# Attention from the 17th block on: one TensorE job per block for scores, query and probability transposes, and a PSUM bank that changes hands

## The chip, the core and the metric

The kernel runs on one core of one Trainium2 chip. The metric is the device time of one execution in microseconds (us); lower is better.

## What is computed

Three stages follow one another. The first is attention over `q`, `k`, `v` of shape (2, 8, 576, 64) that keeps only the 32 largest scores of each row:

```python
scores = scale * np.matmul(q, k.transpose(0, 1, 3, 2))
kth = np.partition(scores, -32, axis=-1)[..., -32:-31]
scores = np.where(scores >= kth, scores, -1e9)
attn = np.exp(scores - scores.max(-1, keepdims=True))
attn = attn / (attn.sum(-1, keepdims=True) + 1e-9)
x = np.matmul(attn, v)
```

The result is seen as 1152 tokens of width 512 (nine tiles of 128). The second stage is a mixture of 8 experts (512 to 1024, ReLU, back to 512), each token weighted by a matrix that eight row and column normalisations make of the gate logits. The third is a mixture of 8 experts in which each token goes to its best expert, with room for 288 tokens per expert. All numbers are float32.

## The kernel before

**A planner writes the order.** Each piece of work is a `Job` with an engine, a rank, a modelled cost, the jobs it depends on, and the buffers (`Box`es of a `Pool`) it takes and uses. `Order.run` (L147) plays the engines forward: it picks the job that can start first and, among those within 0.02 us, the one of lowest rank, and emits its instructions. Every engine then runs its instructions in that order on the chip. A job starts in the plan only when all the boxes in its `take` list are free at once.

**PSUM** has eight banks of 128x512 floats, in two pools (`places`, L297): `psa` for attention and all small work (its tiles are called `tp`), and `psm` for the experts' matmuls (`yp`; `psm` boxes are given out in the order in which they were made). They begin with four banks each. In `visits_first` (L998) one `psa` bank is handed to `psm` and never comes back, so from about 100 us on attention has three banks and the experts five; an expert matmul into that bank shows as `tp` in the profile.

**Attention** is cut into 72 blocks of 128 query rows against 576 keys, for one head (or 64 rows of two heads). Blocks 0 to 15 take another path; from block 16 (`ROWS`) a block n makes these jobs:

- TensorE transposes the query (`block`, one instruction by the helper `tr`, L257) into a bank of its own; ScalarE writes its high part (L598), VectorE the low part (L606). Before that the query is loaded by a DMA of the SP queue.
- Two TensorE jobs make the scores (L618), 288 columns each, each into its own bank; ScalarE copies each to `sc` (L623). Their rank is n-2.
- `search` (L709): VectorE finds the 32nd largest value by four MAX8 and three MATCH_REPLACE8 (L715, L719, L721). After the second round ScalarE writes the exponentials, in halves, into two PSUM banks (L728), and VectorE masks them into `e` (L730). ScalarE divides by the sum (L739).
- Two TensorE jobs transpose `e` (L257): four 128x128 pieces into one bank, the fifth piece into another, at rank n+1. ScalarE writes the high part (L769), VectorE (or GpSimd, for one block in six, later one in three, through a copy on ScalarE) the low part (L773, L777).

So a block has five TensorE jobs and takes seven banks in turn. After the last block of a pair of heads, `values` multiplies by `v` (L809), with one bank per head. `keys` takes two banks per pair.

**The first mixture** is cut into visits (expert, tiles t0 to t1), `visit` (L960). For each of eight slices f, layer 1 (L980) makes a hidden 128 x n tile in a `psm` bank; ScalarE and VectorE read it as two parts (L932, L934); layer 2 (L1090) accumulates into one `psm` bank per tile. The next slice's hidden bank is asked for ahead. The visits in `EARLY` need only tiles that attention has finished and are the work that TensorE does between attention jobs: first 256 columns (two tiles), then two visits of 384, one of 256, two of 512, one of 256. The visits in `LATE` wait for `gate`, which comes after the last block of attention and the gate's logits (L891 to L900); the normalisation (L1138 to L1162) follows.

Of the kernel before, what the change touches and what calls it, by code (L numbers as in the profile page):

```python
# [29 lines left out]
ROWS = 16  # L30
# [182 lines left out]
class Net:  # L213
# [10 lines left out]
    def __init__(self, ctx, tc, q, k, v, wg1, w11, w12, wg2, w21, w22, capacity, out):  # L224
        self.ctx, self.tc, self.nc = ctx, tc, tc.nc
        self.q, self.k, self.v, self.out = q, k, v, out
        self.wg1, self.w11, self.w12 = wg1, w11, w12
        self.wg2, self.w21, self.w22 = wg2, w21, w22
        self.cap = int(capacity)
        self.B, self.H, self.S, self.D = q.shape  # L230
        self.N = self.B * self.S
        self.NT = self.N // 128
        self.E = wg1.shape[1]
        self.F = w11.shape[2]
        self.DM = self.H * self.D
# [5 lines left out]
        self.ending = self.ended = self.fast = False  # L241
        Pool.all, Box.all = [], []


# [177 lines left out]
    def attention(self):  # L422
# [3 lines left out]
        self.khave, self.qhave = {}, {}  # L426
        n = 0
        self.attended = []
        for g, (b, tiles) in enumerate(GROUPS):
            made = []  # L430
            for pair in range(4):
# [12 lines left out]
                    self.block(x)  # L444
                    n += 1
                if n > ROWS:
                    made += self.values(b, pair, tiles, heads, n - 1)
# [4 lines left out]
            self.spans.append((c0, c1, made))  # L452
            for t in range(c0 // 128, -(-c1 // 128)):
                self.xdone.setdefault(t, []).extend(made)
        self.gate_logits()

    def keys(self, b, pair, n):

# [120 lines left out]
    def block(self, x):  # L579
        nc, b, t, pair, n = self.nc, x["b"], x["t"], x["pair"], x["n"]  # L580
        qg, jq = self.queries(b, t, pair, n)
        two = t == 4
        if n < 2:
            return self.block_full(x, qg, jq)
        qs = (self.qz if two else self.qs).box()
        p = self.psa.box()
        i = 0 if two else x["heads"][0]["i"]
        j = self.job("PE", n - 3.5, 0.13, lambda: self.tr(p.t[:, :128], qg.t[:, i].rearrange("p s d -> p (s d)")),
                     deps=[jq], take=[p, qs], use=[qg])

        def parts(s):
            if two:
                return qs.t[:, s].rearrange("p a (c d) -> p (a c) d", c=2)[:, ::3, :]
            return qs.t[:, s]

        def src():
            return p.t[:, :128].rearrange("p (a c) -> p a c", a=2) if two else p.t[:, :128]
        jh = self.job("ACT", n - 2.9, t_act(128), lambda: nc.scalar.activation(parts(0), src(), AF.Copy),  # L598
                      deps=[j], use=[p, qs])
        if 2 <= n < ALONE:  # L600
            jm = self.job("PE", n - 2.9, 0.12, lambda: nc.tensor.matmul(
                p.t[:, :128], self.minus, parts(0), start=False, stop=True, skip_group_check=True), deps=[jh], use=[p, qs])
            jl = self.job("ACT", n - 2.9, t_act(128), lambda: nc.scalar.activation(parts(1), p.t[:, :128], AF.Copy),
                          deps=[jm], use=[p, qs])
        else:
            jl = self.job("DVE", n - 2.4, t_dve(128), lambda: nc.vector.tensor_sub(  # L606
                parts(1), src(), parts(0).bitcast(F32)), deps=[jh], use=[p])
# [3 lines left out]
        got = []  # L611
        for half in range(2):
            ps = self.psa.box()

            def scores(half=half, ps=ps):
                for m, (s, k) in enumerate(terms):
                    w = qs.t[:, s, k, :] if two else qs.t[:, s]
                    nc.tensor.matmul(ps.t[:, :288], w, keys[k][0].t[:, half * 288:(half + 1) * 288],  # L618
                                     start=m == 0, stop=m == len(terms) - 1)
            j = self.job("PE", n - 2 + 0.1 * half, 0.14 * len(terms), scores,  # L620
                         deps=[jh, jl] + [d for _, dd in keys for d in dd], take=[ps] if half else [ps, sc],
                         use=[qs, sc] + [kb for kb, _ in keys])
            got.append(self.job("ACT", n - 1.9 + 0.1 * half, t_act(288), lambda half=half, ps=ps: nc.scalar.activation(  # L623
                sc.t[:, half], ps.t[:, :288], AF.Copy), deps=[j], use=[ps, sc]))
        (self.search_first if n < ROWS else self.search)(x, sc, got)

    def block_full(self, x, qg, jq):

# [80 lines left out]
    def search(self, x, sc, got):  # L709
# [33 lines left out]
        for t0, t1, rows in ((0, 4, 128), (4, 5, 64)):  # L743
            p, nt = self.psa.box(), t1 - t0

            def turn(p=p, t0=t0, t1=t1, rows=rows):
                for t in range(t0, t1):
                    self.tr(p.t[:rows, (t - t0) * 128:(t - t0 + 1) * 128], e.t[:, t * 128:t * 128 + rows])
            fresh = [hd["et"] for hd in heads if "et_done" not in hd]
            for hd in heads:  # L750
                hd.setdefault("et_done", [])
            j = self.job("PE", n + 1, 0.12 * nt, turn, deps=[jn], take=[p] + fresh, use=[e])

            def view(p=p, rows=rows, nt=nt):
                return p.t[:rows, :nt * 128].rearrange("p (t c) -> p t c", t=nt)
            dve = n >= ALONE and n % (EASY if n < 44 else 3)
            if not dve:
                er = self.er.box()

                def copied(er=er, rows=rows, nt=nt):  # L760
                    return er.t[:rows, :nt * 128].rearrange("p (t c) -> p t c", t=nt)
                jr = self.job("ACT", n + 0.6, t_act(128 * nt), lambda p=p, view=view, copied=copied:
                              nc.scalar.activation(copied(), view(), AF.Copy), deps=[j], take=[er], use=[p])
            for i, hd in enumerate(heads):
                def part(s, hd=hd, rows=rows, t0=t0, t1=t1):
                    if s and t0:
                        return hd["et"].t[0][64:, t0:t1, c0:c0 + w]
                    return hd["et"].t[s][:rows, t0:t1, c0:c0 + w]
                jh = self.job("ACT", n + 0.5, t_act(w * nt), lambda i=i, part=part, view=view: nc.scalar.activation(  # L769
                    part(0), view()[:, :, i * w:(i + 1) * w], AF.Copy), deps=[j], use=[p, hd["et"]])  # L770
                if dve:
                    jl = self.job("DVE", n + 0.5, t_dve(w * nt), lambda i=i, part=part, view=view:
                                  nc.vector.tensor_sub(part(1), view()[:, :, i * w:(i + 1) * w], part(0).bitcast(F32)),  # L773
                                  deps=[jh], use=[p])
                else:
                    jl = self.job("POOL", n, t_pool(w * nt), lambda i=i, part=part, copied=copied:
                                  nc.gpsimd.tensor_sub(part(1), copied()[:, :, i * w:(i + 1) * w],  # L777
                                                       part(0).bitcast(F32)), deps=[jh, jr], use=[er])
                hd["et_done"] += [jh, jl]

    def values(self, b, pair, tiles, heads, n):

# [215 lines left out]
    def visits_first(self, count):  # L998
# [26 lines left out]
        for e in range(count):  # L1025
# [741 lines left out]
```

## Time and profile before

| | us |
|---|---|
| median of 3 runs | 1178.45 (1178.33 to 1179.57) |
| the profiled execution's own time | 1180.55 |
| its span, first to last instruction | 1178.8 |
| TensorE busy in the span | 1157.3 (98%) |
| weight loads (PEld) busy | 1003.6 (85%) |
| VectorE busy | 912.8 (77%) |
| ScalarE busy | 734.2 (62%) |

Sums of time below are made against the profiled execution. PE is TensorE's matmuls, whose ends are modelled, so neighbours overlap in the profile and a wait shorter than an overlap does not show as idle; PEld is its weight loads, DVE VectorE, ACT ScalarE, POOL GpSimd, SP the engine whose queue issues most DMAs. PEclk is the granted TensorE clock, 1.00 being 2.4 GHz.

### The profile page before, as it was taken

The page shows a single profiled execution, that of the slowest core. Times are in us where ns is not written, and L with a number is a line of the kernel's source. Part 1 is how long each engine was busy: PE and PEld are TensorE (multiplying, and loading weights), DVE is VectorE, ACT ScalarE, POOL GpSimd, SP SyncE. Part 2 cuts the span into 40 slices and gives each one's busy share as a digit, 9 for nine tenths or more (in the row PEclk, how much of TensorE's full clock was granted, in tenths as well). Part 3 has the DMA queues.
Part 4 walks back from the last instruction along what each step waited for, and adds up shares of the span by engine and source line. Part 5 has one row for each costly group of instructions (what it writes and reads, how often), then busy time and mean ns, then how long its engine had stood idle before and what let it go on. Part 6 is the DMA issues. An engine that isn't in the chain of part 4 may idle for free.

```text
span 1178.8 us, 20927 instructions
## 1 busy us (share of the span) xinstructions
PE 1157.3 (98%) x6610; PEld 1003.6 (85%) x6610; DVE 912.8 (77%) x2194; ACT 734.2 (62%) x1729; POOL 421.2 (36%) x387
## 2 busy tenths in 40 slices
PE   8998999999999999999999999999999999999998
PEld 5876889888888888778888889989999999898886
DVE  7999999999999999995845668754455555568883
ACT  7656888989888978766443335543334444258882
POOL 5463788877556755445000001000000000016541
PEclk9999999999999999999999999999999999999999
DMA  5457765756444664434545555644444444279980
GB/s 142 113 152 196 203 192 174 200 168 165 142 128 113 188 193 131 152 113 147 170 153 180 160 156 185 195 138 122 129 125 143 143 134 135 72 232 359 352 265 23
DMA packets 243032, 194.04 MB, mean 165 GB/s; under 512 B 67487, under 2 KB 186271, under 8 KB 242912
## 3 DMA queue, kind: packets, MB, share of 16 engines
q1 hardware_dynamic: 240656, 187.74, 53.2%
q0 software_dynamic: 1648, 4.73, 1.0%
q8 instruction: 54, 0.88, 0.3%
q14 instruction: 66, 0.54, 0.1%
q10 hardware_dynamic: 608, 0.15, 0.1%
HBM read 172.34 MB, written 20.80 MB: 164 GB/s over the span
## 4 chain that ended last, share of the span: by engine, by line
PE 73%; DVE 15%; ACT 4%; issue 4%; DMA 2%; SPq 1%; POOL 1%; POOLq 0%; DVEq 0%; ACTq 0%
PE yp L980 24%; PE yp L1090 21%; PE tp L1090 6%; PE tp L980 4%; PE tp L257 3%; DVE wk L719 3%; DVE m L721 3%; PE yp L1309 2%; PE tp L618 2%; PE tp L809 2%; DVE wk L665 2%; PE yp L1325 2%; DVE e L730 1%; DVE m L667 1%; PE tp L1309 1%
## 5 line engine op out<-in xcount | busy, mean ns | idle before, releaser
L1718 POOL DMA_INDIRECT disp<-acc,idx x9 | 10.5, 1172 | 460.8 <-DVE run L1714 460.8
L924 POOL TENSOR_TENSOR w0l<-ra,w0h 128x512 fp32r<-128x512 f32 x96 | 124.3, 1295 | 70.8 <-ACT w0h L918 65.0
L924 POOL TENSOR_TENSOR w1l<-rb,w1h 128x512 fp32r<-128x512 f32 x96 | 124.1, 1293 | 61.8 <-ACT w1h L918 56.0
L980 PE MATMUL yp<-xl,w0h 128*128 128x256 f32 (+2 forms) x680 | 142.3, 331 | 0.0
L980 PE MATMUL yp<-xh,w0h 128*128 128x256 f32 (+2 forms) x680 | 141.7, 330 | 0.2 <-ACT w0h L918 0.2
L980 PE MATMUL yp<-xh,w0l 128*128 128x256 f32 (+2 forms) x680 | 141.6, 330 | 0.0
L918 ACT ACTIVATE w0h<-ra 128x512 fp32r<-128x512 f32 x211 | 131.8, 625 | 0.4 <-DMA ra<-in_moe_w_dram 0.3
L918 ACT ACTIVATE w1h<-rb 128x512 fp32r<-128x512 f32 x148 | 93.1, 629 | 55.4 <-PE yp L1090 47.6
L721 DVE MAX8 m<-wk 128x8 f32<-128x576 f32 x168 | 125.8, 756 | 1.0
L980 PEld LDWEIGHTS yp<-xh,w0h 128*128 128x128 f32 x680 | 113.9, 189 | 11.9 <-ACT w0h L918 0.5
L932 ACT ACTIVATE hh<-yp 128x256 fp32r<-128x256 f32 (+3 forms) x142 | 64.0, 450 | 94.8 <-PE yp L980 78.4
L980 PEld LDWEIGHTS yp<-xh,w0l 128*128 128x128 f32 x680 | 110.6, 189 | 6.5 <-POOL w0l L924 0.4
L980 PEld LDWEIGHTS yp<-xl,w0h 128*128 128x128 f32 x680 | 110.9, 190 | 6.0
L1090 PE MATMUL yp<-w1h,hh 128*128 128x512 f32 x280 | 114.3, 408 | 0.0
L934 DVE SCALAR_TENSOR_TENSOR hl<-yp,hh 128x256 fp32r<-128x256 f32 (+3 forms) x142 | 71.8, 506 | 53.5 <-ACT hh L932 52.7
L1090 PE MATMUL yp<-v,f 128*128 128x512 f32 x480 | 111.8, 391 | 0.0
L1090 PE MATMUL yp<-w1l,hh 128*128 128x512 f32 x280 | 110.1, 393 | 0.0
L1090 PE MATMUL yp<-w1h,hl 128*128 128x512 f32 x280 | 109.8, 392 | 0.0
L1090 PEld LDWEIGHTS yp<-v,f 128*128 128x128 f32 x480 | 89.6, 188 | 18.1
L918 ACT ACTIVATE v<-rb 128x512 fp32r<-128x512 f32 x65 | 40.6, 628 | 79.1 <-PE yp L1090 52.4
L719 DVE MATCH_REPLACE8 wk<-m,wk 128x576 f32<-128x576 f32 x112 | 83.7, 748 | 0.5
L921 DVE TENSOR_TENSOR w0l<-ra,w0h 128x512 fp32r<-128x512 f32 x115 | 79.1, 688 | 1.3 <-ACT w0h L918 0.3
(485 smaller groups left out, 2726.9 us busy)
## 6 DMA issues: line engine op xcount, KB each, us to landing
rb<-in_moe_w_dram SPq DMA_DIRECT2D x248, 256.0 KB
ra<-in_moe_w_dram SPq DMA_DIRECT2D x245, 256.0 KB
acc<-in_moe_w_dram SPq DMA_DIRECT2D x67, 256.0 KB
y<-ys SPq DMA_DIRECT2D x31, 256.0 KB
ys<-y SPq DMA_DIRECT2D x21, 256.0 KB
vr<-in_v_dram SPq DMA_DIRECT2D x40, 128.0 KB
disp<-z SPq DMA_DIRECT2D x6, 771.0 KB
qg<-in_q_dram SPq DMA_DIRECT2D x63, 64.0 KB
```

The lines of the kernel that those rows point to most:

```text
L257: self.nc.tensor.transpose(out, in_, self.ident[:p, :p])
L618: nc.tensor.matmul(ps.t[:, :288], w, keys[k][0].t[:, half * 288:(half + 1) * 288], start=m == 0, stop=m == len(terms) - 1)
L719: j = self.job("DVE", r, 0.73, lambda i=i: nc.vector.match_replace(wk.t, m.t[:, i], flat() if i == 0 else wk.t, LOW), deps=[j], take=[wk] ...
L721: j = self.job("DVE", r, 0.66, lambda i=i: nc.vector.max(m.t[:, i + 1], wk.t), deps=[j], use=[wk] if i == 2 else [])
L918: jh = self.job("ACT", -500 + rank, t_act(512, True), lambda r=r, w=w: nc.scalar.activation(w.t[0], r.t, AF.Copy), deps=[j], take=[w])
L921: jl = self.job("DVE", -100 + rank, t_dve(512, True), lambda r=r, w=w: nc.vector.tensor_sub(w.t[1], r.t, w.t[0].bitcast(F32)), deps=[jh], ...
L924: jl = self.job("POOL", -100 + rank if k > 8 * NATIVE + 4 else FIRST - 3, t_pool(512), lambda r=r, w=w: nc.gpsimd.tensor_sub(w.t[1], r.t, ...
L932: jh = self.job("ACT", -1000 + k * 0.001, t_act(b - a), lambda: nc.scalar.activation(h.t[0][:, a:b], p.t[:, :b - a], AF.Relu), deps=deps, ...
L934: jl = self.job("DVE", -1000 + k * 0.001, t_dve(b - a), lambda: nc.vector.scalar_tensor_tensor(h.t[1][:, a:b], p.t[:, :b - a], 0.0, h.t[0] ...
L980: nc.tensor.matmul(p.t[:, :b - a], w1[0].t[i][:, d, :], self.xt[s][:, d, c0 + a:c0 + b], start=m == 0 and d == 0, stop=m == 2 and d == 3)
L1090: nc.tensor.matmul(y[t].t, h.t[i][:, c:c + 128], w2[0].t[s], start=f == 0 and m == 0, stop=f == last and m == 2)
L1309: nc.tensor.matmul(p.t[:, :n], w1[0].t[i][:, d, :], hl.t[s][:, d, :n], start=m == 0 and d == 0, stop=m == 2 and d == 3)
```

## The change

From block 19 on, the TensorE work of a block is not five jobs but is collected into one job by a new method `together(m)`: the scores of block m+3 (both halves), the transpose of the query of block m+4, then the five transposes of `e` of block m. The job has all their dependencies and takes all their boxes at once. The query's transpose goes to columns 288 to 415 of the bank of the second half of the scores, the fifth transpose of `e` to the same columns of the bank of the first half. The job thus takes three banks, and a block five in all with the two of the exponentials, which stay in PSUM. The making of `values` is put off until the pair's last block has its job.

The bank that `psa` gives to `psm` in `visits_first` is given back at the end of `visits_first`; the first early visit of 512 columns takes it again. Between the two, attention has four banks and the experts four. The modelled cost of a transpose of `e` goes from 0.12 to 0.11 us. The instructions, their sizes and the DMAs stay the same.

```diff
+AHEAD = 3
+GROUPED = AHEAD + 1
...
+        for m in range(n - GROUPED, n):
+            self.together(m)
...
+    def together(self, m, query=None):
+        turn, rows = self.turns.get(m), self.rows_.pop(m + AHEAD, None)
+        if turn:
+            deps, take, use, cost, tail, _, jobs = turn
+            calls = []
+            tail.append(rows[2][0] if rows else self.psa.box())
+            take = take + ([] if rows else tail)
+            use = use + tail
+            if rows:
+                x, sc, ps, sdeps, stake, suse, scores, _ = rows
+                deps, take, use, cost = deps + sdeps, take + stake, use + suse, cost + 0.14 * 4 * len(x["heads"])
+                calls.append(scores)
+            go = jobs[0]
+            if query:
+                qdeps, qtake, quse, *_ = query
+                deps, take, use, cost = deps + qdeps, take + qtake, use + quse, cost + 0.13
+            def all_(calls=calls, go=go, query=query):
+                for f in calls:
+                    f()
+                if query:
+                    query[3]()
+                go()
+            j = self.job("PE", m, cost, all_, deps=deps, take=take, use=use)
...
@@ block
-        p = self.psa.box()
+        mine = n >= ROWS + GROUPED
+        p, at = (None, 288) if mine else (self.psa.box(), 0)
...
+        if n < ROWS + AHEAD:
...
+            return (self.search_first if n < ROWS else self.search)(x, sc, got)
...
+            bank[0] = self.rows_[n - 1][2][1]
+            query = [jq], [qs], [qg, qs], turn_q, split_q
+        if mine:
+            self.together(n - GROUPED, query)
+        self.rows_[n] = (x, sc, banks, mid + [d for _, dd in keys for d in dd], [*banks, sc],
+                         [qs, sc] + [kb for kb, _ in keys], lambda: [scores(0), scores(1)], finish)
...
@@ search
+        def turn():
+            for t in range(5):
+                rows, o, b = (128, t * 128, p) if t < 4 else (64, 288, tail[0])
+                self.tr(b.t[:rows, o:o + 128], e.t[:, t * 128:t * 128 + rows])
...
+        self.turns[n] = [[jn], [p] + fresh, [e], 0.11 * 5, tail, (None, None), (turn, split)]
...
@@ visit
+        if n == 512 and early and not self.wide:
+            self.wide, back = True, self.psa.box()
+            self.job("X", 0, 0.0, lambda: self.psm.free.append((self.o.t["PE"], back.t)),
+                     deps=[self.chain[t] for t in self.chain], take=[back])
...
@@ visits_first, at its end
+        lent = self.psm.box()
+        self.job("X", 0, 0.0, lambda: self.psa.free.append((self.o.t["PE"], lent.t)), deps=[done], take=[lent])
```

## Rows read from the trace of the kernel before

**Rows 1.** The page's first part: busy time and share of each engine.

```profile
PE 1157.3 (98%) x6610; PEld 1003.6 (85%) x6610; DVE 912.8 (77%) x2194; ACT 734.2 (62%) x1729; POOL 421.2 (36%) x387
```

**Rows 2.** Busy time by stretch; columns: stretch, length, engines, clock, DMA.

```profile
100.00:120.00 20.00, 16.57 (x90) 12.87 (x91) 17.26 (x41) 14.81 (x44) 10.66 (x12) 0.91 0.74 199
120.00:291.00 171.00, 169.32 (x1111) 150.62 (x1111) 167.58 (x461) 151.56 (x388) 136.52 (x124) 1.00 0.66 184
291.00:382.00 91.00, 90.25 (x511) 79.62 (x511) 89.19 (x233) 74.74 (x188) 56.52 (x55) 1.00 0.46 131
382.00:415.00 33.00, 32.58 (x217) 28.96 (x216) 32.68 (x88) 29.66 (x79) 24.36 (x24) 1.00 0.61 175
415.00:545.00 130.00, 128.79 (x682) 105.09 (x682) 126.28 (x343) 99.44 (x249) 64.06 (x63) 1.00 0.46 147
545.00:570.00 25.00, 24.26 (x154) 21.44 (x153) 14.75 (x51) 12.50 (x26) 11.44 (x13) 1.00 0.52 158
570.00:1003.00 433.00, 433.00 (x2228) 385.31 (x2227) 252.40 (x506) 180.68 (x342) 7.63 (x6) 1.00 0.49 151
```

**Rows 3.** Timeline of PE, 200 to 208 us: start, length, what, count.

```profile
200.25 0.27 PE L257 MATMUL tp<-ident,qg 128*128 128x128 f32 x1
...
200.60 0.39 PE L1090 MATMUL yp<-w1l,hh 128*128 128x512 f32 x1
...
203.19 0.70 PE L618 MATMUL tp<-kst,qs 128*128 128x288 f32 x4
203.72 0.40 PE L1090 MATMUL yp<-w1h,hh 128*128 128x512 f32 x1
...
206.65 0.71 PE L257 MATMUL tp<-ident,e 128*128 128x128 f32 x5
...
207.43 0.39 PE L1090 MATMUL yp<-w1l,hh 128*128 128x512 f32 x1
```

**Rows 4.** Groups of weight loads (PEld), 100 to 545 us: busy, mean, idle before.

```profile
L257 PEld LDWEIGHTS tp<-ident,e 128*128 128x128 f32 (+1 forms) x280 | 31.6, 134 | 12.1 <-ACT e L739 2.4 <-DVE xr L814 1.3 <-DVE e L730 0.9
L618 PEld LDWEIGHTS tp<-kst,qs 128*128 128x128 f32 x184 | 29.4, 190 | 10.1 <-ACT sc L623 2.2 <-DVE e L730 1.4 <-DVE etl L773 1.4
...
L618 PEld LDWEIGHTS tp<-kst,qz 128*128 128x128 f32 x64 | 9.2, 188 | 2.1 <-DVE eth L773 0.8 <-DVE etl L773 0.7 <-DVE qs L606 0.2
...
L257 PEld LDWEIGHTS tp<-ident,qg 128*128 128x128 f32 x52 | 7.3, 141 | 7.3 <-DVE eth L773 2.7 <-DVE etl L773 1.3 <-DVE qs L606 1.0
```

**Rows 5.** Groups of the 384-column visits, 291 to 382 us, by form.

```profile
L934 DVE SCALAR_TENSOR_TENSOR hl<-yp,hh 128x384 fp32r<-128x384 f32 x12 | 6.6, 549 | 0.0
L932 ACT ACTIVATE hh<-yp 128x384 fp32r<-128x384 f32 x12 | 5.8, 487 | 3.2 <-PE yp L980 3.1
```

**Rows 6.** Groups of ACT and DVE that hold attention's banks, 100 to 545 us, by form.

```profile
L918 ACT ACTIVATE w0h<-ra 128x512 fp32r<-128x512 f32 x93 | 58.2, 625 | 0.1
L728 ACT ACTIVATE tp<-sc,st 128x288 f32<-128x288 f32 x110 | 55.0, 504 | 14.1 <-DVE e L730 7.4 <-DVE etl L773 2.5 <-DVE st L738 1.3
L623 ACT ACTIVATE sc<-tp 128x288 f32<-128x288 f32 x109 | 43.2, 406 | 5.6 <-PE tp L618 5.0
L769 ACT ACTIVATE eth<-tp 128x512 fp32r<-128x512 f32 x48 | 28.6, 596 | 5.1 <-PE tp L257 4.7
...
L721 DVE MAX8 m<-wk 128x8 f32<-128x576 f32 x165 | 123.5, 756 | 0.9
L730 DVE SCALAR_TENSOR_TENSOR e<-sc,m,tp 128x288 f32<-128x288 f32 x110 | 54.4, 508 | 1.0 <-ACT tp L728 0.6
L606 DVE TENSOR_TENSOR qs<-tp,qs 128x128 fp32r<-128x128 f32 x45 | 12.6, 281 | 0.0
```

**Rows 7.** Timeline of PE: first 512-column early visit, gate's last transposes, first late visit.

```profile
415.05 1.09 PE L980 MATMUL yp<-xh,w0h 128*128 128x512 f32 x4
...
554.07 0.49 PE L257 MATMUL tp<-ident,lgt 128*128 128x128 f32 x3
...
568.35 1.07 PE L980 MATMUL yp<-xh,w0h 128*128 128x512 f32 x4
```

More of the change, by code (lines that the diff above doesn't have):

```diff
@@ L240, in __init__ @@
         self.outs, self.moves = [], []
-        self.ending = self.ended = self.fast = False
+        self.ending = self.ended = self.fast = self.wide = False
         Pool.all, Box.all = [], []
@@ L428, in attention @@
         self.attended = []
+        self.turns, self.rows_, self.late = {}, {}, []
+        late = self.late
         for g, (b, tiles) in enumerate(GROUPS):
@@ L446, in attention @@
                 if n > ROWS:
-                    made += self.values(b, pair, tiles, heads, n - 1)
+                    late.append((n - 1, lambda b=b, pair=pair, tiles=tiles, heads=heads, n=n, made=made:
+                                 made.extend(self.values(b, pair, tiles, heads, n - 1))))
                 else:
@@ L452, in attention @@
             self.spans.append((c0, c1, made))
+        for m in range(n - GROUPED, n):
+            self.together(m)
+        for c0, c1, made in self.spans:
             for t in range(c0 // 128, -(-c1 // 128)):
@@ L455, in attention @@
         self.gate_logits()
+    def together(self, m, query=None):
[21 more added lines that the diff above has]
+            j = self.job("PE", m, cost, all_, deps=deps, take=take, use=use)
+            if query:
+                query[4](j)
+            jobs[1](j)
+            if rows:
+                rows[7](j)
+        while self.late and self.late[0][0] <= m:
+            self.late.pop(0)[1]()
     def keys(self, b, pair, n):
@@ L585, in block, with turn_q @@
         qs = (self.qz if two else self.qs).box()
-        p = self.psa.box()
+        mine = n >= ROWS + GROUPED
+        p, at = (None, 288) if mine else (self.psa.box(), 0)
+        bank = [p]
         i = 0 if two else x["heads"][0]["i"]
-        j = self.job("PE", n - 3.5, 0.13, lambda: self.tr(p.t[:, :128], qg.t[:, i].rearrange("p s d -> p (s d)")),
-                     deps=[jq], take=[p, qs], use=[qg])
+        mid = []
+        def turn_q():
+            self.tr(bank[0].t[:, at:at + 128], qg.t[:, i].rearrange("p s d -> p (s d)"))
         def parts(s):
@@ L596, in src, with split_q @@
         def src():
[L597 to L607, printed above, removed]
+            v = bank[0].t[:, at:at + 128]
+            return v.rearrange("p (a c) -> p a c", a=2) if two else v
+        def split_q(j):
+            p = bank[0]
+            jh = self.job("ACT", n - 2.9, t_act(128), lambda: nc.scalar.activation(parts(0), src(), AF.Copy),
+                          deps=[j], use=[p, qs])
+            if 2 <= n < ALONE:
+                jm = self.job("PE", n - 2.9, 0.12, lambda: nc.tensor.matmul(
+                    p.t[:, :128], self.minus, parts(0), start=False, stop=True, skip_group_check=True), deps=[jh], use=[p, qs])
+                jl = self.job("ACT", n - 2.9, t_act(128), lambda: nc.scalar.activation(parts(1), p.t[:, :128], AF.Copy),
+                              deps=[jm], use=[p, qs])
+            else:
+                jl = self.job("DVE", n - 2.4, t_dve(128), lambda: nc.vector.tensor_sub(
+                    parts(1), src(), parts(0).bitcast(F32)), deps=[jh], use=[p])
+            mid.extend([jh, jl])
         terms = [(s, k) for s in range(2) for k in range(len(x["heads"]))]
@@ L610, in block @@
         sc = self.sc.box()
[L611 to L624, printed above, removed]
@@ L625, in block, with scores, copied @@
-        (self.search_first if n < ROWS else self.search)(x, sc, got)
+        banks = [self.psa.box() for _ in range(2)]
+        def scores(half):
+            ps = banks[half]
+            for m, (s, k) in enumerate(terms):
+                w = qs.t[:, s, k, :] if two else qs.t[:, s]
+                nc.tensor.matmul(ps.t[:, :288], w, keys[k][0].t[:, half * 288:(half + 1) * 288],
+                                 start=m == 0, stop=m == len(terms) - 1)
+        def copied(half, j):
+            return self.job("ACT", n - 1.9 + 0.1 * half, t_act(288), lambda: nc.scalar.activation(
+                sc.t[:, half], banks[half].t[:, :288], AF.Copy), deps=[j], use=[banks[half], sc])
@@ new lines, in finish @@
+        def finish(j):
+            (self.search_first if n < ROWS else self.search)(x, sc, [copied(half, j) for half in range(2)])
+        if n < ROWS + AHEAD:
+            split_q(self.job("PE", n - 3.5, 0.13, turn_q, deps=[jq], take=[p, qs], use=[qg]))
+            got = []
+            for half in range(2):
+                j = self.job("PE", n - 2 + 0.1 * half, 0.14 * len(terms), lambda half=half: scores(half),
+                             deps=mid + [d for _, dd in keys for d in dd], take=[banks[1]] if half else [banks[0], sc],
+                             use=[qs, sc] + [kb for kb, _ in keys])
+                got.append(copied(half, j))
+            return (self.search_first if n < ROWS else self.search)(x, sc, got)
@@ new lines, in block @@
+        query = None
+        if not mine:
+            split_q(self.job("PE", n - 3.5, 0.13, turn_q, deps=[jq], take=[p, qs], use=[qg]))
+        else:
+            bank[0] = self.rows_[n - 1][2][1]
[4 more added lines that the diff above has]
+                         [qs, sc] + [kb for kb, _ in keys], lambda: [scores(0), scores(1)], finish)
@@ L627, in block_full @@
+        return
     def block_full(self, x, qg, jq):
@@ L742, in search @@
         w = 128 // len(heads)
[L743 to L779, printed above, removed]
```

34 lines of the change are left out of this document (added).

## The prediction

> **What bounds the kernel now.** I read the page's totals first: TensorE is busy for 98% of the span, the next engine, VectorE, for 77% [rows 1]. Then the stretches. From 570 to 1003 us TensorE does not idle at all, so whatever reaches that point earlier ends earlier; VectorE has 180 of 433 us free there. Between 100 and 545 us, where attention and the early visits run together, two engines are full at once: TensorE idles 445 - 437.5 = 7.5 us by its matmul rows, VectorE is busy for 433.0 of 445 us, and each waits for the other through ScalarE [rows 2]. The end of the kernel therefore moves by what TensorE's idle time before 570 us changes, as long as early visits last; what attention gains in itself is worth nothing. The last transposes of the gate's logits start at 554.07 and the first late visit at 568.35, so attention may slip by some 14 us before TensorE runs out of early work [rows 7].
>
> **The matmul work itself.** Does one job in place of five save TensorE time? From 200.25 to 200.60 one query transpose and one 512-column matmul pass, from 206.65 to 207.43 five transposes and one such matmul: 0.35 and 0.78, so four more transposes cost 0.43, a transpose 0.108 and the matmul 0.24. A transpose that stands alone costs no more than one in a row of five. Four score matmuls take 203.72 - 203.19 = 0.53, 0.133 each, between matmuls of other kinds [rows 3]. Going from one kind of work to another has no price that these rows show, so gathering saves 0 here, and no instruction is added or taken away. The DMAs are the same and pass nothing on the SP queue. The cost of 0.11 in place of 0.12 in the plan is nearer to 0.108, and what it changes is 53 x 5 x 0.01 = 2.7 us of modelled time: it is spread over the order, 0 in the sum.
>
> **The waits that go.** What is left is idle time. By the weight-load rows from 100 to 545 us the query transposes have 7.3 us of idle before them, the score matmuls 10.1 + 2.1, the transposes of `e` 12.1 [rows 4]; together 31.6. Most of that hides under the matmul before it, as only 7.5 us of idle show in the matmul rows [rows 2]. After the change the query and the scores no longer stand alone in the queue: their inputs were made in the job one block before, so the group waits for the normalised `e` and for its banks, as the transposes of `e` do now. I let the wait of `e` stay and take 7.3 + 10.1 + 2.1 = 19.5 us of load waits away. Their share of the visible idle is 7.5 x 19.5 / 31.6 = 4.6 us; the upper bound is 19.5, if every one delayed a matmul; the lower bound is 0, as these waits may only move to the group. I take 5, next to the matmul rows, since they are the nearest to what delays the end: **-5 us**. In the 20 us from 100 to 120 the granted clock is 0.91 of 2.4 GHz, so some of it ran at the lower level of 1.2 GHz, with 3.4 us of idle in the matmul rows [rows 2]; the changed blocks begin only inside this stretch, so I count nothing for the clock, and 20 x 0.09 = 1.8 us remain as a bound on the gain side.
>
> **The banks.** A group takes three banks at once, and the plan cannot start it before all three are free. It holds them for 0.53 + 0.11 + 5 x 0.108 = 1.18 us of TensorE, then two score copies of 0.41, a high part of 0.60 and two small ones of some 0.28 each, taking the query's low part for their length, and a last low part of 0.28: about 1.18 + 1.98 + 0.28 = 3.4, or 4.1 with one weight conversion of 0.63 ahead of it on ScalarE. The exponentials hold two banks for 2 x 0.50 + 2 x 0.51 = 2.0 us at least, and 3.5 if the last search round of two times about 0.75 falls between [rows 6]. VectorE does three later MAX8 per block, so 445 / (165 / 3) = 8.1 us is a block's period [rows 6]. With four banks, until the first 512-column visit at 415 us [rows 7], 4.1 + 3.5 fits with room. With three banks, from 415 to 545 us, group and exponentials exclude each other, and 7.6 of 8.1 us leaves little for `keys` and `values`. The scores stand three blocks ahead, so VectorE has other blocks to search while a group is late: I cost this at 0, covered by those blocks and by the 14 us; the price without that cover is the rival below.
>
> The expert side pays: between the two loans it has four banks. A visit of 256 columns uses two for its sums and keeps two hidden banks, nothing lost. A visit of 384 uses three and keeps one, so layer 1 of the next slice must wait until ScalarE (0.49) and VectorE (0.55) have read the hidden tile [rows 5]. TensorE's cover is layer 2 of the slice before, nine matmuls of 512 columns, 9 x 0.24 = 2.2 us [rows 3]. Bare, the reads take 1.04 and fit; with one foreign operation ahead on each engine (0.63 and 0.76) they take 2.43 and stick out by 0.25, before any hand-over [rows 6]. For two visits of eight slices that is 0 to 16 x 0.25 = 4, or 8 with hand-overs of another 0.25. What queues behind the waiting layer 1 is all of TensorE's order, the next group with it, and behind that ScalarE's copies. I take 16 x 0.12 = **+2 us**, as the other attention work of TensorE, 1.2 of every 8.1 us, falls into part of these gaps.
>
> The low parts and copies that now read a shared bank keep their lengths. VectorE's low parts wait little today: its masks idle 1.0 us in 110 operations, the query's low parts 0.0 in 45 [rows 6]. The Trainium skill (PSUM — Partial Sum Buffer, section "PSUM bank collisions raise a hardware error") says that two engines must not be in one bank at once, whatever columns they use; by it the query's low part and the score copy next to it have to take turns, and so have the copy and the low part of the fifth piece of `e`. That speaks against this change, and it is a rival below. In the sum I put 0, as the copies come first in ScalarE's order and VectorE has a longer low part to do before.
>
> **The sum.** -5 + 2 = -3 on the execution of 1180.55, which is 2.1 above the median of 1178.45: 1177.5 there, **1175.5** against the median. The likeliest case has a range of its own of 1171 to 1176.
>
> **The rivals.**
>
> 1. *No difference.* The idle of TensorE is the pace of VectorE and ScalarE: in this stretch VectorE has 12 of 445 us free [rows 2], and a group that waits for the last of all its inputs waits as long as five jobs did in all. For it: both engines are full. Against it: 19.5 of 31.6 us of load waits stand before work that will have been ready for a block. It holds also if the planner finds no four free banks and the order hardly changes. Time 1178.5, within 0.2% (2.4 us, about what a measurement of this kernel can tell from no change).
> 2. *Attention falls behind in the three-bank stretch.* Place: 415 to 545 us, 130 / 8.1 = 16 blocks. If group and exponentials stop overlapping and `keys` and `values` come between, each block may take 1.5 us longer: 24 us, less the slack of 14, is 10 us in which TensorE has neither early nor late visits: 1188.5. It decides from 14 / 16 = 0.9 us per block on. For it: 7.6 of 8.1 us. Against it: banks are freed one by one and the halves of the exponentials take one each.
> 3. *Turns in the shared banks.* If VectorE waits for a score copy of 0.41 once per block, half of it unhidden, 53 x 0.2 = 11 us are lost on VectorE, and as TensorE waits for VectorE in turn, some 7 of them, beyond the gain of 3, arrive: 1182.5. By the skill's rule named above such turns are forced, and no row before shows this pair of operations in one bank.
> 4. *The one hidden bank.* All 8 us of the upper bound, less 5: 1181.5.
> 5. *Nearly all waits go*, with half of the load waits reaching the end: about -10, 1168.5.
>
> **How the numbers follow.** The forecast gets 0.42, the large gain 0.07, no difference 0.22, falling behind 0.15, the turns 0.09, the one hidden bank 0.05. So faster by over 0.2% 0.49, the same 0.22, slower 0.29. The time is the likeliest case's, 1175.5. The range of 8 in 10 goes from 1167, past the large gain, to 1187, which leaves out the worse half of falling behind.
>
> **What would show it.** Right: one run of scores, query and `e` transposes per block in TensorE's timeline; idle before query and score weight loads near 0; matmul idle from 100 to 545 us of 2 to 4 in place of 7.5; the first late visit at about 565. Wrong: idle before layer 1 in the 384-column visits over 4 us (the one hidden bank); the gate's last transposes after 565 and idle before the first late visit (falling behind); VectorE's low parts waiting for score copies (the turns); waits before `e` grown by what the others lost (no difference). If TensorE's time per transpose or score differs between alone and grouped, my first step is wrong, and the gain would be larger than all of this.

## The result: 1.3% slower, and the profile after

The changed kernel takes 1194.91 us (median of 4 runs, 1193.35 to 1195.67) against 1179.01 for the kernel before beside it: a ratio of 1.0133, 95% interval 1.0121 to 1.0146. The profiled execution took 1193.35 us, 12.8 more than the one before. The forecast was 1175.5.

The busy time by stretch up to 600 us, with the bounds of [rows 2] (columns: stretch, length, busy time and count of PE, PEld, DVE, ACT, POOL, granted clock, DMA share, GB/s):

```profile
100.00:120.00 20.00, 15.95 (x99) 11.21 (x98) 16.17 (x42) 14.63 (x39) 10.62 (x12) 1.00 0.76 199
120.00:291.00 171.00, 167.42 (x1108) 152.31 (x1107) 160.60 (x430) 146.14 (x380) 134.21 (x121) 1.00 0.65 183
291.00:382.00 91.00, 89.67 (x514) 80.58 (x513) 89.50 (x237) 71.48 (x186) 55.06 (x55) 1.00 0.47 131
382.00:415.00 33.00, 32.49 (x213) 29.04 (x212) 30.67 (x86) 29.78 (x75) 26.95 (x24) 1.00 0.67 192
415.00:545.00 130.00, 127.83 (x670) 106.53 (x669) 121.75 (x317) 94.02 (x241) 63.06 (x64) 1.00 0.48 149
545.00:570.00 25.00, 24.96 (x157) 20.64 (x155) 24.06 (x59) 20.44 (x49) 12.14 (x11) 1.00 0.57 180
570.00:600.00 30.00, 27.08 (x130) 20.68 (x129) 17.24 (x66) 8.37 (x18) 1.29 (x5) 0.94 0.15 43
```

From 100 to 545 us VectorE is busy for 418.7 us where it was 433.0: attention is 14 us of VectorE's work behind. That work comes after 545 us, where VectorE now has 24.06 of 25 us against 14.75 [rows 2]. More than half of the 14 us is in the first two rows already (1.1 + 7.0), up to 291 us.

TensorE seems as busy as before, but part of it is not work. Line 296 multiplies a tile of ones (`ones_b`), a filler that the planner puts where TensorE has nothing to do (line 294 before, with no filler after 113.2 us). In the trace of after, the fillers in attention's banks (`tp`) and, last, those of the start (`yp`):

```profile
L296 PE MATMUL tp<-ones_b x48: 379/379/634, 413.9 to 580.2; 128*128 128x512 bf16 x48
L296 PE MATMUL yp<-ones_b x41: 379/380/634, 3.3 to 114.1; 128*128 128x512 bf16 x41
```

TensorE's timeline shows where these 48 stand: first ahead of the first 512-column visit, then between the last early and the first late visit. [rows 7] has the same places before the change.

```profile
413.86 0.82 PE L296 MATMUL tp<-ones_b 128*128 128x512 bf16 x3
...
415.73 1.24 PE L296 MATMUL tp<-ones_b 128*128 128x512 bf16 x5
418.34 0.39 PE L885 MATMUL tp<-eth,vs 128*128 128x256 f32 x1 [1.37 <-DVE etl L848]
...
419.52 1.90 PE L296 MATMUL tp<-ones_b 128*128 128x512 bf16 x8
...
422.40 1.08 PE L1060 MATMUL tp<-xh,w0h 128*128 128x512 f32 x4
...
565.17 0.39 PE L1172 MATMUL yp<-w1h,hl 128*128 128x512 f32 x1
565.59 0.66 PE L259 MATMUL tp<-ident,e 128*128 128x128 f32 x4
...
566.19 4.05 PE L296 MATMUL tp<-ones_b 128*128 128x512 bf16 x18
572.65 1.12 PE L259 MATMUL yp<-ident,e 128*128 128x128 f32 x4 [2.40 <-ACT e L809]
...
573.77 2.23 PE L296 MATMUL tp<-ones_b 128*128 128x512 bf16 x5
...
578.49 2.12 PE L296 MATMUL tp<-ones_b 128*128 128x512 bf16 x9
...
582.56 0.27 PE L259 MATMUL tp<-ident,lgt 128*128 128x128 f32 x1
582.59 1.17 PE L1060 MATMUL tp<-xh,w0h 128*128 128x512 f32 x4
```

At the first 512-column visit: 0.82 + 1.24 + 1.90 = 4.0 us of fillers and 1.4 of idle. The visit starts only at 422.40, behind the `values` (row at 418.34) and the gate's logits of tiles that attention finished late. At the end: the last early layer 2 ends at 565.56, the first late visit starts at 582.59, and two blocks of attention, `values` and the gate's logits lie between with 4.05 + 2.23 + 2.12 = 8.4 us of fillers and some 3 us of idle (25 + 30 - 24.96 - 27.08). Together about 17 us lost; the first late visit comes 14.2 us later than before [rows 7], and the end 12.8 later.

How late attention is shows in the first MAX8 of a block's search. The 18th search from the end and the last one, before:

```profile
399.66 0.74 DVE L715 MAX8 m<-sc 128x8 f32<-128x576 f32 x1
...
527.23 0.75 DVE L715 MAX8 m<-sc 128x8 f32<-128x576 f32 x1
```

and after:

```profile
414.18 0.74 DVE L785 MAX8 m<-sc 128x8 f32<-128x576 f32 x1
...
556.13 0.74 DVE L785 MAX8 m<-sc 128x8 f32<-128x576 f32 x1
```

The lag is 14.5 us where the four-bank stretch ends and 28.9 at the end. Counted in the same way it was 18.8 at 290 us (search at 290.07 against 271.32) and 8.2 at 357 (356.70 against 348.55): attention falls behind up to 291 us, makes up half of it in the 384-column visits, and falls behind again.

The waits that the forecast was about did go. The weight loads of attention, 100 to 545 us, that had 31.6 us of idle before them [rows 4] (last column: idle before):

```profile
L259 PEld LDWEIGHTS tp<-ident,e 128*128 128x128 f32 (+1 forms) x197 | 21.9, 135 | 0.1
L667 PEld LDWEIGHTS tp<-kst,qs 128*128 128x128 f32 x131 | 21.3, 188 | 6.1 <-ACT sc L671 1.3 <-DVE kst L569 1.1 <-DVE e L800 0.8
L667 PEld LDWEIGHTS yp<-kst,qs 128*128 128x128 f32 x52 | 8.6, 188 | 2.1 <-DVE e L800 0.9 <-DVE eth L848 0.6 <-ACT sc L671 0.3
...
L259 PEld LDWEIGHTS tp<-ident,qg 128*128 128x128 f32 x34 | 4.8, 140 | 0.0
L667 PEld LDWEIGHTS yp<-kst,qz 128*128 128x128 f32 x20 | 3.0, 188 | 1.1 <-DVE e L800 0.8 <-DVE qz L655 0.3
```

With the groups left out (0.0, 0.3, 0.0) that is 9.7 us. They came back on VectorE. Its groups in the same stretch that waited little before:

```profile
L785 DVE MAX8 m<-sc 128x8 f32<-128x576 f32 x53 | 39.7, 748 | 6.9 <-ACT sc L671 6.9
...
L848 DVE TENSOR_TENSOR etl<-tp,eth 128x512 fp32r<-128x512 f32 x26 | 17.7, 680 | 5.8 <-ACT eth L844 5.8
...
L655 DVE TENSOR_TENSOR qs<-tp,qs 128x128 fp32r<-128x128 f32 x29 | 8.2, 283 | 3.5 <-ACT qs L647 3.3
```

These idle for 16.2 us; the same three kinds idled for 2.2 before. A search waits for the copy of its scores, which comes late because the group that makes them came late, or because ScalarE copies them late; the two-job run below has the numbers for both.

### The profile page after: what moved, and what is told of

It is laid out like the page before. It is cut to its first block, busy times and chain, and to the rows that moved or that the text cites. A ratio compares the mean times of both kernels' runs of the same rounds, so it can differ in the third digit from the quotient of the medians.

```text
span 1191.5 us, 20988 instructions
## 1 busy us (share of the span) xinstructions
PE 1163.5 (98%) x6659; PEld 1012.4 (85%) x6659; DVE 916.9 (77%) x2194; ACT 730.0 (61%) x1729; POOL 421.1 (35%) x387
## 4 chain that ended last, share of the span: by engine, by line
PE 63%; DVE 21%; ACT 8%; issue 5%; POOL 1%; DMA 1%; SPq 1%; POOLq 0%; DVEq 0%; ACTq 0%
PE yp L1172 15%; PE yp L1060 14%; PE tp L1060 10%; PE tp L1172 9%; DVE m L791 4%; DVE wk L789 4%; DVE e L800 2%; PE tp L259 2%; DVE hl L1010 2%; PE tp L1391 2%; DVE wk L735 1%; PE yp L1391 1%; DVE m L737 1%; DVE etl L848 1%; DVE m L785 1%
## 5 line engine op out<-in xcount | busy, mean ns | idle before, releaser
L1060 PE MATMUL yp<-xh,w0h 128*128 128x256 f32 (+2 forms) x496 | 98.5, 320 | 1.9 <-ACT w0h L994 1.5
L1060 PE MATMUL yp<-xl,w0h 128*128 128x256 f32 (+2 forms) x496 | 98.3, 320 | 0.0
L1060 PE MATMUL yp<-xh,w0l 128*128 128x256 f32 (+2 forms) x496 | 98.0, 319 | 0.0
L1060 PEld LDWEIGHTS yp<-xh,w0h 128*128 128x128 f32 x496 | 81.8, 188 | 11.4 <-ACT w0h L994 2.4
L1172 PE MATMUL yp<-v,f 128*128 128x512 f32 x360 | 84.4, 391 | 0.0
L1060 PEld LDWEIGHTS yp<-xh,w0l 128*128 128x128 f32 x496 | 79.0, 189 | 3.1 <-POOL w0l L1000 0.3
L1060 PEld LDWEIGHTS yp<-xl,w0h 128*128 128x128 f32 x496 | 79.0, 189 | 2.5
L1172 PEld LDWEIGHTS yp<-v,f 128*128 128x128 f32 x360 | 67.2, 188 | 13.5
L1008 ACT ACTIVATE hh<-yp 128x256 fp32r<-128x256 f32 (+3 forms) x105 | 44.7, 426 | 43.9 <-PE yp L1060 28.3
L1060 PE MATMUL tp<-xh,w0h 128*128 128x384 f32 (+2 forms) x304 | 66.1, 339 | 0.9 <-DVE hl L1010 0.9
```

The costliest lines, as they stand in the source:

```text
L1008: jh = self.job("ACT", -1000 + k * 0.001, t_act(b - a), lambda: nc.scalar.activation(h.t[0][:, a:b], p.t[:, :b - a], AF.Relu), deps=deps, ...
L1060: nc.tensor.matmul(p.t[:, :b - a], w1[0].t[i][:, d, :], self.xt[s][:, d, c0 + a:c0 + b], start=m == 0 and d == 0, stop=m == 2 and d == 3)
L1172: nc.tensor.matmul(y[t].t, h.t[i][:, c:c + 128], w2[0].t[s], start=f == 0 and m == 0, stop=f == last and m == 2)
```

## The experiments

Theory **A**: the time is lost where early visits run out before the gate is done. **A1**: attention is late because three free banks at once are rare, as other jobs take each bank as it comes free. Rivals for the lateness: **A2**, the order (scores queue behind the normalised `e`), **A3**, ScalarE and VectorE taking turns in the shared banks, and the loan. All ratios are against the kernel before on the same chip.

### One more early visit, in the changed kernel and in the one before

```diff
-EARLY = [... (4, 2, 6), (0, 4, 6)]
-LATE = [(5, 2, 6), (6, 2, 6), (7, 2, 6), (1, 4, 6), (2, 4, 6)] + ...
+EARLY = [... (4, 2, 6), (0, 4, 6), (1, 4, 6)]
+LATE = [(5, 2, 6), (6, 2, 6), (7, 2, 6), (2, 4, 6)] + ...
```

In the changed kernel:

> The changed kernel with one late visit (expert 1, tiles 4 and 5, 256 columns, some 23 us of TensorE work) moved to the end of the early visits; attention untouched. Theory A (the loss is the gap at the end of attention: early visits are used up at 565 us, the gate's logits come at 582, and TensorE has no expert work in between): the gap of some 17 us is filled, of which 5 us was attention's own work; time 1181 to 1184, with two more tiles parked. Theory B (the loss is spread over the groups, as waits of TensorE inside 100 to 565 us): the gap is filled with work that is then missing nowhere, time stays 1192 or more.

1182.88 us (1181.08 to 1184.57), ratio 1.0026 (1.0016 to 1.0036): 12.0 us back, with attention no earlier (the gate's last transposes at 581.75). No filler is left after 420.2 us:

```profile
L296 PE MATMUL tp<-ones_b x16: 379/379/390, 413.0 to 420.2; 128*128 128x512 bf16 x16
```

So A holds for most of the loss: it is the gap at the end. In the kernel before:

> The kernel before with the same visit moved. Control for the run above: TensorE had no gap at the end of attention, so both theories expect 1178 to 1181, the cost of parking two more tiles being all that can show.

1189.3 us (1186.79 to 1191.41), ratio 1.0070 (1.0049 to 1.0091): a miss, as no change was expected. The gate's last transposes start at 554.15, as before (554.07), but the visit now runs beside the normalisation, whose small matmuls wait for VectorE where they waited 0.3 us:

```profile
L1162 PE MATMUL tp<-prob,ones 128*128 128x72 f32 x16 | 3.1, 276 | 7.3 <-DVE prob L1152 7.3
```

and the stretch from 570 to 600 us runs at a granted clock of 0.89. From 545 to 600 us TensorE idles for 7.8 us in place of 0.7 [rows 2]. An early visit more costs 9.5 us where there is no gap to fill. With that visit in both, the changed kernel is the faster one, by 6.4 us: what the change costs depends on how much early work there is.

### The group cut in two: three banks at once, or two and then one more

The first job makes the scores and the query (two banks), the second the transposes of `e` (a third bank; the fifth piece still goes to the first's). The first keeps the group's wait for the normalised `e`, so the order, the sharing and the loan stay as in the change.

```diff
-                deps, take, use, cost = deps + sdeps, take + stake, use + suse, cost + 0.14 * 4 * len(x["heads"])
+                sdeps, stake, suse, scost = deps + sdeps, list(stake), list(suse), 0.14 * 4 * len(x["heads"])
...
-            j = self.job("PE", m, cost, all_, deps=deps, take=take, use=use)
+                js = self.job("PE", m, scost, first, deps=sdeps, take=stake, use=suse + ps[1:])
+            j = self.job("PE", m, cost, jobs[0], deps=deps + [js], take=take, use=use)
```

> The changed kernel with the group cut in two jobs: scores and query first (two banks), then the five transposes of e (one bank, and columns of a bank that the first holds). Both still wait for the normalised e, and the banks are shared as in the change; only the taking of three banks at once is undone. Theory A1 (attention is late because three free banks at once are rare): attention is back near its old pace, gate's logits before 568 us, no gap, time at most 1182. Theory A2 (late because the scores stand behind the normalised e): still late, 1190 or more. Theory A3 (late because VectorE and ScalarE take turns in the shared banks): still late, 1190 or more.

1177.59 us (1175.55 to 1178.93), ratio 0.9980 (0.9970 to 0.9989): 17.3 us less than the changed kernel, the gate's last transposes at 561.20, and no filler after 114.8 us. The first group shows why. The changed kernel's timeline, 102 to 120 us (all engines; the lines picked normalise `e`, or take or hold attention's banks):

```profile
102.09 0.77 ACT L809 ACTIVATE e<-e,st 128x576 f32<-128x576 f32 x1
...
105.42 0.98 ACT L798 ACTIVATE tp<-sc,st 128x288 f32<-128x288 f32 x2
...
106.57 0.66 PE L555 MATMUL tp<-ident,kg 128*128 128x128 f32 x4 [0.49 <-ACT lgt L970]
...
107.07 0.27 PE L259 MATMUL yp<-ident,kg 128*128 128x128 f32 x1
...
108.71 0.33 PE L259 MATMUL tp<-ident,lgt 128*128 128x128 f32 x1
...
109.35 0.27 PE L259 MATMUL tp<-ident,lgt 128*128 128x128 f32 x1
...
115.76 0.51 ACT L798 ACTIVATE tp<-sc,st 128x288 f32<-128x288 f32 x1 [0.23 <-DVE kst L569]
...
116.55 0.23 DVE L569 TENSOR_TENSOR kst<-yp,kst 64x64 fp32r<-64x64 f32 x1
...
117.95 1.07 PE L667 MATMUL tp<-kst,qs 128*128 128x288 f32 x4
118.86 0.27 PE L259 MATMUL tp<-ident,qg 128*128 128x128 f32 x1
118.97 0.71 PE L259 MATMUL tp<-ident,e 128*128 128x128 f32 x5
```

and the same block in two jobs:

```profile
102.44 0.77 ACT L806 ACTIVATE e<-e,st 128x576 f32<-128x576 f32 x1
104.15 0.74 PE L664 MATMUL tp<-kst,qs 128*128 128x288 f32 x4
104.73 0.27 PE L259 MATMUL tp<-ident,qg 128*128 128x128 f32 x1
104.84 0.60 PE L259 MATMUL yp<-ident,e 128*128 128x128 f32 x4
```

In two jobs `e` is normalised at 103.21 and transposed at 104.84. In one, it is ready at 102.86 and is transposed at 118.97: exponentials, keys, the gate's logits and the next exponentials each take one or two banks in between, and the group starts only at 117.95. The keys hold their two banks longest, from 106.57 and 107.07 until VectorE has read the second one at 116.78.

The first group is among the longest waits. In two jobs the second group waits for 8.4 us too. Over all 53 groups that make scores, from the end of the normalisation of `e` to the first score matmul in the timelines, the mean is 4.2 us in the changed kernel (5.6 up to 291 us, 1.7 up to 415, 4.8 behind it) and 1.8 in two jobs (2.5, 0.6, 1.9). This is A1, with the order on TensorE, the sharing and the loan unchanged.

The run changes one thing more. In two jobs ScalarE may copy the scores before `e` is transposed, and from a group's first score matmul to the first copy it is 1.8 us on average, against 3.3 in the changed kernel. So the 17.3 us are shown for one job against two; how they divide between the late group and the late copy is not shown.

The second form drops the first job's wait for `e`, which is what A2 is about:

```diff
-                sdeps, stake, suse, scost = deps + sdeps, list(stake), ...
+                sdeps, stake, suse, scost = list(sdeps), list(stake), ...
```

> The two-job kernel in which the first job (scores and query) no longer waits for the normalised e of the block three behind. Theory A2 says that this order is what makes attention late: then 3 us or more below the 1177.6 of the two-job kernel. Theory A1: within 2 us of it, as the scores stand three blocks ahead of their search.

1176.03 us (1175.43 to 1178.09), ratio 0.9963 (0.9954 to 0.9973): the order is worth some 1.6 us of the 17 to 19. This is the fastest version, 4 us faster than the kernel before. Its first late visit starts at 563.69 in place of 568.35.

### The loan

Without the loan, in the changed kernel (three banks throughout):

```diff
-        if n == 512 and early and not self.wide:
-            self.wide, back = True, self.psa.box()
...
-        lent = self.psm.box()
-        self.job("X", 0, 0.0, lambda: self.psa.free.append((self.o.t["PE"], lent.t)), deps=[done], take=[lent])
```

> The changed kernel without the loan of the bank: attention has three banks from about 100 us to its end, the experts five, the group takes three at once. Theory A1 (three free banks at once are rare): groups now wait in the stretch from 105 to 410 us as they do behind it, gate's logits later than 582 us, time 1195 to 1205, less at most 5 for the pause at 414 to 422 us that the return of the bank brings. If the loan itself were the loss: 1180 to 1185.

1194.86 us (1193.51 to 1195.36), ratio 1.0119 (1.0102 to 1.0136): no difference from the changed kernel. The expectation puts the pause at 414 to 422 us down to the return of the bank. That is wrong, as the pause is there without the loan, and so are the fillers at the end, until 581.0:

```profile
412.75 2.33 PE L296 MATMUL yp<-ones_b 128*128 128x512 bf16 x10
...
416.43 2.33 PE L296 MATMUL yp<-ones_b 128*128 128x512 bf16 x10
```

The first 512-column visit starts at 421.38 here: it waits for late attention, as the first late visit does. The two-job form without the loan:

> The two-job kernel (scores and query, then e) without the loan. It ran at 1177.6 with it. If two jobs do not need the fourth bank: 1176 to 1180. If the blocks wait for banks even in two takes when only three are there: gate's logits later than 565 us and 1182 or more.

1188.09 us (1186.56 to 1189.70), ratio 1.0065 (1.0045 to 1.0085), 10.5 us worse than with it, with 21 fillers from 413.7 us on at the same place. And the loan alone in the kernel before:

> The kernel before with the loan alone: four banks for attention and four for the experts between 103 and 415 us, five jobs per block as before. Theory A1: the loan is not what costs; 1177 to 1182. If four expert banks cost (the one hidden bank of the 384-column visits, or the return of the bank): 1184 or more.

1180.14 us (1178.84 to 1181.44), ratio 1.0002 (0.9992 to 1.0012). In its stretch of 384-column visits, with one hidden bank, TensorE has 89.78 of 91 us against 90.25 [rows 2]:

```profile
291.00:382.00 91.00, 89.78 (x510) 78.47 (x509) 89.97 (x239) 75.28 (x193) 54.69 (x55) 1.00 0.46 128
```

This run also measures the slack. VectorE has done 5.5 us less from 120 to 291 us than before (162.08 against 167.58), and the gate's last transposes start at 561.23, 7.2 us later; yet the first late visit starts at 568.22, as before, and no time is lost.

So lending costs the experts nothing that can be measured; a fourth bank is worth nothing to five small jobs, 10 us to two jobs, and nothing that can be measured to one job that wants three.

### Two jobs apart, the scores one block nearer, exponentials in SBUF

The two jobs with no tie between them (from the fastest version: the fifth piece of `e` in a bank of its own, the scores half a block later in rank):

```diff
-            tail.append(rows[2][0] if rows else self.psa.box())
-            take = take + ([] if rows else tail)
+            tail.append(self.psa.box())
+            take = take + tail
...
-                js = self.job("PE", m, scost, first, ...)
-            j = self.job("PE", m, cost, jobs[0], deps=deps + [js], ...)
+                js = self.job("PE", m + 0.5, scost, first, ...)
+            j = self.job("PE", m, cost, jobs[0], deps=deps, ...)
```

> The changed kernel with the group cut into two jobs that have nothing to do with each other: scores with the query (two banks, half a block lower in rank), and the five transposes of the normalised exponentials, whose fifth piece gets a bank of its own again (two banks). The query still shares a bank with the scores. The loan stays. If what helped the two-job forms (1177.6 and 1176.0 us) is only that no job asks for three banks at once: within 2 us of 1176. If the one bank per block saved by sharing earns something of its own: 1178 to 1183, with the gate's logits over 2 us later than 561.6 us. If turns between ScalarE and VectorE in the bank of the fifth piece cost: 1172 to 1175.

1178.85 us (1177.24 to 1180.76), ratio 0.9990 (0.9980 to 0.9999), the gate's last transposes at 565.64 against 561.39 in the fastest version: the tie and the shared bank are worth about 2.8 us. Which of the two, and the rank, this run does not separate. If turns in the shared bank of the fifth piece were dear, this form would have gained. In the first two-job form the turns that VectorE waits for can be seen, and are small (last column: idle, and what ended it):

```profile
L652 DVE TENSOR_TENSOR qs<-tp,qs 128x128 fp32r<-128x128 f32 x38 | 10.7, 283 | 2.0 <-ACT qs L644 1.3 <-ACT sc L668 0.5
```

0.5 us in 38 low parts is put down to the score copy in the same bank. The turns that ScalarE waits for are larger. Its score copies in the changed kernel, 100 to 545 us:

```profile
L671 ACT ACTIVATE sc<-tp 128x288 f32<-128x288 f32 x74 | 28.9, 406 | 3.9 <-DVE eth L848 1.5 <-DVE qs L655 1.3 <-DVE qz L655 0.7
```

With 2.1 us for the copies from `yp`, 5.6 us of ScalarE's idle time end with a low part that VectorE reads in a shared bank; before, 5.0 of 5.6 us ended with the scores themselves [rows 6]. In the first two-job form it is 3.0 us. As that form shares the banks too and is fast, the turns alone are not the loss; whether they have a part in it was not tried.

The changed kernel with `AHEAD = 2`:

> The changed kernel with its groups as they are but the scores two blocks ahead instead of three (one constant). Theory: a late group is hidden as long as VectorE has searches of already scored blocks before it; with two blocks ahead there is one block less, 8 us, to hide the wait for three banks, so VectorE idles before its first MAX8 of a block and the gate's logits come well later than 582.6 us: over 590, time 1203 to 1240. Rival: the blocks ahead do not matter, since banks set the pace of all groups alike: within 3 us of 1194.9, gate's logits 580 to 586.

One run, 1225.47 us: 30 us slower than with three blocks, the gate's last transposes at 614.45. The searches' wait for their scores grows from 6.9 to 10.9 us, that of the query's low parts from 3.5 to 9.2. The blocks ahead do cover late groups, only not enough of them. What a block less costs without groups was not tried.

The changed kernel with the exponentials in SBUF, so that no bank is taken for them:

```diff
-            p = self.psa.box()
-            je = self.job("ACT", ..., activation(p.t[:, :288], sc.t[:, half], AF.Exp, ...))
+            je = self.job("ACT", ..., activation(e.t[:, h], sc.t[:, half], AF.Exp, ...))
-                e.t[...], sc.t[:, half], m.t[:, 3, 7:8], p.t[:, :288], op0=OP.is_ge, ...
+                e.t[:, h], sc.t[:, half], m.t[:, 3, 7:8], e.t[:, h], op0=OP.is_ge, ...
```

> The changed kernel with the exponentials written to e in SBUF and masked there in place, so that a block takes three banks in all instead of five; the group is as in the change. Theory A1 (banks are short): the groups find their three banks sooner, time at most 1183. Theories A2 and A3 (order, or turns in shared banks): 1190 or more, as neither is touched.

1211.27 us (1206.94 to 1213.01), ratio 1.0258 (1.0227 to 1.0288): a miss, and it says little of the banks, as the mask became dearer:

```profile
L800 DVE SCALAR_TENSOR_TENSOR e<-sc,m,e 128x288 f32<-128x288 f32 x100 | 84.5, 875 | 0.5
```

875 ns in place of 508 [rows 6], 0.37 us twice a block, 41 us in 56 blocks of an engine that is full here. The Trainium skill (Vector Engine (DVE) Microarchitecture Reference, section "7. Points that are easy to get wrong") says that this operation runs at half throughput with two sources in SBUF that are not bf16; the rows agree in direction, at 1.7 times the duration.

## Why the prediction was wrong

- **The matmul work itself: right.** The five transposes in a group take 0.71 us (row at 118.97) as they did [rows 3], and gathering saves none of TensorE's work.
- **The waits that go: right in mechanism, not in where they went.** 31.6 us of load waits fell to 9.7, more than the 19.5 taken away, as the waits of `e` went too. But the forecast counted them as gone; in the grouped form 14 us of waits appeared on VectorE. Only in the two-job forms does a gain reach the end, at most 4.1 us by the medians in the fastest version (load waits 18.2), beside the 5 expected. Some of it may be the clock, which the prediction bounded at 1.8 us and left out: from 100 to 120 us it is granted at 1.00 there, not 0.91 [rows 2].
- **The banks: this step failed.** "With four banks ... 4.1 + 3.5 fits with room" compared the time for which banks are held with the period of a block. That counts banks as if any free one would do. A job that needs three at the same moment waits until three coincide, and jobs that need one keep breaking the coincidence: 16.1 us from `e` to its transposes for the first group, and 4.2 us on average from `e` to the scores, where two jobs have 1.8. Keys, the gate's transposes and the exponentials broke it at the first group, in the four-bank stretch; the prediction had weighed `keys` and `values` only where there are three.
- **"I cost this at 0, covered by those blocks and by the 14 us": mis-sized.** The term is 17.3 us (one job against two). The blocks ahead are a real cover, 30 us for the third, and so is the slack, which was sized well: the last search starts 29 us later, and 14.2 of these reach the first late visit.
- **The one hidden bank, +2 us:** about 0, by the loan alone.
- **Turns in shared banks, 0:** about right for VectorE's low parts (0.5 us of waits in 38 in the two-job form), but the reason given, that "the copies come first in ScalarE's order", did not hold. In the changed kernel's first group ScalarE writes the high parts of `e` at 120.56 and of the query at 121.71, and copies the scores at 122.21, after waiting for the low part of the fifth piece. The Trainium skill (PSUM — Partial Sum Buffer, section "PSUM bank collisions raise a hardware error") forbids two engines in one bank at once; the trace agrees that both sides wait for each other, 5.6 us in the score copies.
- **The rivals.** "Attention falls behind" named the mechanism that came, with its sign (the idle before the first late visit, the gate after 565), but placed it from 415 to 545 us alone and priced it at 1188.5. Half of it is there: from 415 us to the last search a block takes 8.4 us in place of 7.5, the 0.9 from which the rival decides, and the lag grows from 14.5 to 28.9 us. The other half comes with four banks: from 100 to 291 us the kernel starts 22 searches in place of 25. Together they go beyond the slack, and the first 512-column visit has to wait as well, with a pause of some 5 us. The range, up to 1187, left out the half of this rival that came true.

What stays open: how much of the 14 us on VectorE is the late group and how much the late copy, as each group hands ScalarE five pieces at once (two copies, a query part, two parts of `e`).

## What to carry to other kernels

A job that takes several buffers at one moment is not as cheap as the same buffers taken one after another: beside jobs that take one, it waits until enough are free together, and the sum of holding times against the period does not show it. Gather work by order, but let each part take its buffers when it needs them. And when a stage has filler work to hide its lateness, measure the slack first: here the same 12 us could be hidden by one more early visit, which cost 9.5 us in the kernel that had no gap.

## What the runs showed of the hardware that was not expected

- VectorE's mask on 128x288 floats takes 508 ns with one of its two inputs in PSUM and 875 ns with both in SBUF. In the run one of them was also its output; whether that has a part in it was not tried.
- From 116 to 120 us the kernel before has a granted clock of 0.59, so most of it ran at the lower of the levels of 1.2 and 2.4 GHz, after 8 us in which TensorE was busy for 2.81 + 2.28 us, with two waits of 1.2 us among its rows. The fastest version, busy for 2.49 + 3.42 us there, kept 1.00, and so did the changed kernel with 2.54 + 2.92 us. The fall is worth 4 x 0.41 = 1.6 us of TensorE at most. By stretch, in the kernel before:

```profile
108.00:112.00 4.00, 2.81 (x19) 2.39 (x19) 2.97 (x8) 3.08 (x11) 1.00 (x2) 1.00 0.46 127
112.00:116.00 4.00, 2.28 (x12) 1.41 (x11) 3.94 (x11) 1.99 (x6) 0.69 (x1) 0.99 0.95 245
116.00:120.00 4.00, 4.00 (x20) 3.81 (x20) 2.73 (x5) 2.87 (x8) 3.92 (x4) 0.59 0.91 247
```
